# Issuing the tail products of an attention group as one team of eight on TensorE

## The chip, the cores and the metric

The program runs on one core of a Trainium2 chip. The metric is device time in microseconds (us) from one launch; lower is better. TensorE (PE in the profile) does the matrix products, ScalarE (ACT) the Tanh, Exp and copies, VectorE (DVE) additions and conversions, GpSimd (POOL) a little, and SyncE (SP) issues the transfers.

## What is computed

Three stages follow each other. The change is in the first.

```python
# 4 batches, 12 heads, 448 positions, 64 per head
scores = scale * (q @ k.T); scores = cap * tanh(scores / cap)
attn = exp(scores - max) / (sum + 1e-9);  x = attn @ v
...
# second stage: 4 experts, each a causal attention over x, mixed by a gate's top 2
# third stage: x @ w_in, GELU, normalisation, a product over positions, x + gated @ w_out
```

## The kernel before, in words

Heads are worked in 24 **pairs** (4 batches of 6); two pairs are a **group**. Positions 0 to 383 of the keys are three blocks of 128, and 384 to 447 are a tail of 64. Per pair and block, `block` makes the scores (tile `s{b}_{pair}_{c}`, c = 0 to 2): a product for each of the two heads, 64 rows deep and 128 columns wide, side by side on the upper and lower half of TensorE (the profile writes 64\*128). `tails` makes the scores of the tails of a whole group at once (`s{b}_{pair}_3`): four products of 64\*64, one on each quarter of the array. ACT turns scores into probabilities `p`: a Tanh from PSUM, then an Exp in place. `values` multiplies them by v: per pair six products of 128\*64 into `po`, two side by side. The value products of the tails (`po<-p,vt`) are again four of 64\*64: t = 0 on the upper two quarters, into the first pair's `po`, and t = 1 on the lower two, into the second pair's. `sums` adds rows (128\*32).

`slot(i)` records pair i's scores and pair i-1's values. Before the change, the tail scores of group (i, i+1) are the end of `scores(..., 1)` in an even slot i, and the tail values of group (i-2, i-1) stand at the head of `values` for pair i-1, in the same slot. All of it is recorded in the class `Agenda` and issued in an order that a planner makes from fixed costs: `order` takes, step by step, the instruction that can begin first. In slots from 10 on, second-stage work is recorded between the pairs; the first ten slots also prepare w_in (`w2ps` products of 128\*128, fed by VectorE). From pair 12 on the block scores are three single-pass products each (`qh`, `ql`, `kh`, `kl`).

A **team** is a run of recorded PE products of one shape that lie on different cells of the array; the first of them waits until all inputs of the team from outside are there, and has to find buffers for all. The others don't repeat that test (`begin`, lines 275 to 288):

```python
            if i in gang and gang[i][0] == i:
                mates = gang[i]
                wait = first[i]
...
            t = max(t, ready[i])
```

A float32 product is two instructions on PE (two passes), so a row of the profile with x4 is two products. Row names leave buffer numbers out.

Of the kernel before, what the change touches and what calls it, by code (L numbers as in the profile page):

```python
# [10 lines left out]
F32 = mybir.dt.float32  # L11
# [5 lines left out]
AF = mybir.ActivationFunctionType  # L17
# [4 lines left out]
B, H, S, D = 4, 12, 448, 64  # L22
HP = H // 2
# [5 lines left out]
KB, KT = 3, 64  # L29
# [12 lines left out]
def drain(gen):  # L42
    for _ in gen:
        pass
# [32 lines left out]
class Agenda:  # L77


    LATENCY = {"pe": 230.0, "act": 60.0, "dve": 60.0, "pool": 100.0, "sp": 60.0}  # L80
    SLACK, MARGIN = 1000.0, (150.0, 200.0)
    STATE = ("slots", "queue", "where", "left", "free", "grid", "fresh", "cfg", "bank", "lock", "pipe", "kept")
    RULES = ((100.0, 0.0, 100.0), (100.0, 0.0, None), (100.0, 20.0, 100.0), (60.0, 0.0, 100.0))
    OVERLAP = {"act": 100.0, "dve": 80.0, "pool": 27.0, "sp": 0.0}
# [47 lines left out]
    def add(self, eng, f, args, kw):  # L132
        i, name = len(self.ops), f.__name__
# [7 lines left out]
        after, tiles = set(), []  # L141
        for x, wr in [(x, False) for x in ins] + [(x, True) for x in outs]:
            t = x.tensor
# [13 lines left out]
        for these, those in self.behind.items():  # L157
            if any(x.startswith(these) for x in tiles):
                after.update(self.of[those])
        op = dict(i=i, eng=eng, call=lambda: f(*args, **kw), after=after, tiles=set(tiles), took=[], port=False,  # L160
                  rank=i + self.late)
        n = max(x.free_size() for x in ins[:2] + outs[:1])
        psum = any(x.space == PSUM for x in ins + outs)
# [8 lines left out]
        elif eng == "pe":  # L172
            st, mv = (args[1], args[1]) if name == "transpose" else (kw.get("lhsT", args[1]), kw.get("rhs", args[-1]))
            n = mv.free_size() if name != "transpose" else args[1].partition_size()
# [3 lines left out]
            r, c = half(st.partition_size()), half(outs[0].partition_size())  # L178
            if name == "transpose":
                r = c = 4  # L180
# [23 lines left out]
    def order(self, new, by_level, floor):  # L204
        ops, uses = self.ops, self.uses
        then = {i: [] for i in range(len(ops))}
# [3 lines left out]
        for i in reversed(new):  # L210
            op = ops[i]
            took = op["dur"] + self.LATENCY[op["eng"]]
            if "bytes" in op:
                took = 2100.0 + op["extra"] + op["pipe"]
            elif op["eng"] == "pe":
                took = op["dur"] + (0.0 if any(ops[j]["eng"] == "pe" for j in then[i]) else 220.0)
# [4 lines left out]
        for t, u in uses.items():  # L221
            left[t] = len({i for i in u if "end" not in ops[i]}) + (t in keep)
            if t in self.kept and not left[t] and where.get(t, (0, None))[1] is not None:
                key, s = where[t]
                slots[key][s] = max(ops[j]["end"] for j in u)
        self.kept = keep
        for key, tiles in self.caps.items():
# [5 lines left out]
            for t in old:  # L233
                s = next((s for s, v in enumerate(slots[key]) if v is not None), None)
# [24 lines left out]
        gang, team = {}, []  # L259
        for i in new:  # L260
            op = ops[i]
            if op["eng"] != "pe":
                continue
            r, c, r0, c0 = op["cell"]
            if (r, c) == (4, 4) or not team or (r, c) != ops[team[0]]["cell"][:2] or any(
                    abs(r0 - ops[j]["cell"][2]) < r and abs(c0 - ops[j]["cell"][3]) < c for j in team):
                team = []
            team.append(i)
            gang[i] = team
# [46 lines left out]
        while todo:  # L316
            best = None
            for e, pool in pools.items():
# [13 lines left out]
                if e == "pe":  # L332
                    t, i = max(near, key=lambda x: (ops[x[1]]["bank"] == self.bank, ops[x[1]]["key"], -x[1]))
                elif e == "sp":
                    t, i = min(near, key=lambda x: x[1])
                else:
                    t, i = max(near, key=lambda x: (ops[x[1]]["key"], -x[1]))
# [3 lines left out]
            t, i = best  # L341
            op = ops[i]
            e = op["eng"]
            pools[e].remove(i)
            for x in op["tiles"]:
                key, s = where.get(x, (None, 0))
                if s is not None or x not in queue[key]:
                    continue
                s = min((v, k) for k, v in enumerate(slots[key]) if v is not None)[1]
# [4 lines left out]
            if e == "pe":  # L354
                r, c, r0, c0 = op["cell"]
# [25 lines left out]
            for x in op["tiles"]:  # L381
                left[x] -= 1
                if not left[x] and x in where:
                    key, s = where[x]
# [35 lines left out]
def build(ctx: ExitStack, tc: tile.TileContext, a: dict):  # L420
# [145 lines left out]
    def halves(i, c):  # L566
        return (slice(0, S // 2), slice(S // 2, S)) if i == c == 0 else (slice(0, S),)

    def block(s, c, qp, kp, i):

        q, k = parts.get(i, ((qp,), (kp,)))
        of = [(k[0], q[0]), (k[0], q[-1]), (k[-1], q[0])][:1 if len(q) == 1 else 3]
        for n, (y, x) in enumerate(of):
            for o in halves(i, c):
                for j in range(2):
                    r = slice(64 * j, 64 * j + 64)
                    mm(s[:, j, o], y[r, c * 128:(c + 1) * 128], x[r, o], start=(n == 0), stop=(n == len(of) - 1))

    def tails(s, *of):

        for w, (qp, kp) in enumerate(of):
            for j in range(2):
                r = slice(64 * j, 64 * j + 64)
                mm(s[64 * w:64 * w + 64, j, :S], kp[r, KB * 128:S], qp[r, :], start=True, stop=True)

    def scores(b, hp, h, qp, kp, then=None):


        n = 1 if h and then is None else 2
        p = at.tile([128, 2, 2, S], F32, tag="p", name=f"p{b}_{hp}_{h}", bufs=4)
        for c2 in range(n):
            s = ps_s.tile([128, 2, 512], F32, tag="s", name=f"s{b}_{hp}_{2 * h + c2}")
            if 2 * h + c2 < KB:
                block(s, 2 * h + c2, qp, kp, b * HP + hp)
            else:
                tails(s, (qp, kp), then)
            for o in halves(b * HP + hp, 2 * h + c2):
                act.activation(p[:, :, c2, o], s[:, :, o], AF.Tanh, scale=tsc)  # L600
            yield 805.0


        act.activation(p[:, :, :n, :], p[:, :, :n, :], AF.Exp, scale=capt)
        if h == 0:
            pb = at.tile([128, 2, S], F32, tag="pb", name=f"pb{b}_{hp}", bufs=3)
            (dve if (b, hp) < (4, 0) else pool_e).tensor_tensor(pb, p[:, :, 0, :], p[:, :, 1, :], op=ALU.add)
            pend[b, hp] = (p, pb)
        else:
            p0, pb = pend[b, hp]  # L610
            pend[b, hp] = (p0, p, pb)
            if n == 2:
                ptail[b, hp // 2] = p[:, :, 1, :]

    def add_up(b, hp):
# [2 lines left out]
        r = slice(64 * (hp % 2), 64 * (hp % 2) + 64)  # L618
        dve.tensor_tensor(pb[r], pb[r], ptail[b, hp // 2][r], op=ALU.add)

    def values(b, hp, vv):


        i, w = hp // 2, hp % 2
        if w == 0:
            po = ps_o.tile([128, 512], F32, tag="po", name=f"po{b}_{hp}")
            for c in range(KB):
                for j in range(2):
                    mm(po[64 * j:64 * j + 64, :S], vv[:, j, c, :], pend[b, hp][c // 2][:, j, c % 2, :],
                       start=(c == 0), stop=False)  # L630
                yield 805.0
            po_t[b, i] = po
            return
        po = (po_t.pop((b, i)), ps_g.tile([128, 512], F32, tag="g", name=f"po{b}_{hp}"))
        v, p = vt.pop((b, i)), ptail.pop((b, i))
        for t in range(2):
            r = slice(64 * t, 64 * t + 64)
            for j in range(2):
                mm(po[t][64 * j:64 * j + 64, :S], v[r, j, :], p[r, j, :], start=(t == 1), stop=(t == 0))
        yield 805.0  # L640
        os_t[b, i] = ao.tile([128, 2, S], F32, tag="os", name=f"os{b}_{hp}", bufs=5)
        act.activation(os_t[b, i][:, 0, :], po[0][:, :S], AF.Copy)
        for c in range(KB):
            for j in range(2):
                mm(po[1][64 * j:64 * j + 64, :S], vv[:, j, c, :], pend[b, hp][c // 2][:, j, c % 2, :],
                   start=False, stop=(c == KB - 1))
            yield 805.0
        act.activation(os_t[b, i][:, 1, :], po[1][:, :S], AF.Copy)
# [26 lines left out]
    def slot(i, side):  # L675

        if i == 0:
            ld[0] = load_pair(*pairs[0])  # L680
            ld[1] = load_pair(*pairs[1])
        if i + 2 < len(pairs):
            qk = [at.tile([128, n], F32, tag=t, name=f"{t}{i + 2}", bufs=3) for t, n in (("qp", S), ("kp", S + 1))]
            b, hp = pairs[i + 2]
            dma(qk[1][:, :S], a["kT"][b, :, hp, :])
            dma(qk[0], a["qT"][b, :, hp, :])
            ld[i + 2] = qk
        part(i + 1)
        if i < len(pairs):
            first = scores(*pairs[i], 0, *ld[i][:2])  # L690
            drain(islice(first, 2))
            side("a")
            drain(first)
        else:
            side("a")
        side("w")
        if i:
            b, hp = pairs[i - 1]
            drain(values(b, hp, ld.pop(i - 1)[2]))
        if 0 < i < len(pairs) - 1:  # L700
            b, hp = pairs[i + 1]
            ld[i + 1] = (*ld[i + 1], load_v(b, hp))
        side("a")
        if i < len(pairs):
            drain(scores(*pairs[i], 1, *ld[i][:2], None if i % 2 else ld[i + 1][:2]))
        if i == len(pairs):
            drain(sums(B - 1, HP // 2 - 1))
            spread(B - 1, HP // 2 - 1)
        side("p")
        if 0 < i < len(pairs):  # L710
            b, hp = pairs[i - 1]
            if hp % 2 == 1:
                drain(sums(b, hp // 2))
        if i < len(pairs):
            add_up(*pairs[i])
        side("n")
# [726 lines left out]
```

## Time and profile before

| what | us |
|---|---|
| median of 3 runs | 492.72 (492.25 to 493.89) |
| the profiled execution | 492.94 |
| its span, first to last instruction | 491.1 |
| outside the span | 1.84 |
| PE busy | 484.3 (99%) |

The span is what the trace shows; what lies around it stays the same for a kernel with the same launch. PE's granted clock is 1.000 over the span, its full 2.4 GHz.

### The profile page before, as it was taken

The page shows a single profiled execution, that of the slowest core. Times are in us where ns is not written, and L with a number is a line of the kernel's source. Part 1 is how long each engine was busy: PE and PEld are TensorE (multiplying, and loading weights), DVE is VectorE, ACT ScalarE, POOL GpSimd, SP SyncE. Part 2 cuts the span into 40 slices and gives each one's busy share as a digit, 9 for nine tenths or more (in the row PEclk, how much of TensorE's full clock was granted, in tenths as well). Part 3 has the DMA queues.
Part 4 walks back from the last instruction along what each step waited for, and adds up shares of the span by engine and source line. Part 5 has one row for each costly group of instructions (what it writes and reads, how often), then busy time and mean ns, then how long its engine had stood idle before and what let it go on. Part 6 is the DMA issues. An engine that isn't in the chain of part 4 may idle for free.

```text
span 491.1 us, 7664 instructions
## 1 busy us (share of the span) xinstructions
PE 484.3 (99%) x2723; PEld 332.8 (68%) x2723; DVE 362.2 (74%) x796; ACT 325.1 (66%) x555; POOL 47.8 (10%) x61
## 2 busy tenths in 40 slices
PE   9999999999999999999999999999999999999996
PEld 3333333456556657675658797687898998999996
DVE  4999999777899898998756789729979929707000
ACT  6999968999869887788736766647555625513201
POOL 0000000000200303100201302033010200100000
PEclk9999999999999999999999999999999999999999
DMA  8986556555161624141046320161010110110122
GB/s 285 351 308 186 168 133 184 174 151 168 42 176 43 191 61 155 50 131 40 33 128 193 93 81 33 45 240 50 0 39 1 39 37 1 56 57 19 57 75 75
DMA packets 37301, 53.38 MB, mean 109 GB/s; under 512 B 7696, under 2 KB 32272, under 8 KB 37264
## 3 DMA queue, kind: packets, MB, share of 16 engines
q1 hardware_dynamic: 36832, 52.56, 33.9%
q8 instruction: 21, 0.34, 0.3%
q10 hardware_dynamic: 432, 0.34, 0.2%
q14 instruction: 16, 0.13, 0.1%
HBM read 41.97 MB, written 10.83 MB: 108 GB/s over the span
## 4 chain that ended last, share of the span: by engine, by line
PE 90%; DVE 4%; ACT 3%; DMA 1%; issue 1%; SPq 0%; ACTq 0%
PE o L449 18%; PE po L449 12%; PE qk L449 12%; PE s L449 11%; PE sp L449 7%; PE v L449 7%; PE a L449 4%; PE hv L449 4%; PE hu L449 4%; PE w2ps L449 4%; PE av L449 3%; PE tr L449 3%; ACT p L449 2%; PE sum L449 2%; DMA wi_0w<-in_w_in_dram 1%; DVE pb L449 1%
## 5 line engine op out<-in xcount | busy, mean ns | idle before, releaser
L449 ACT ACTIVATE p<-s,tsc 128x896 f32<-128x896 f32 (+1 forms) x85 | 82.3, 999 | 13.1 <-PE s L449 13.0
L449 ACT ACTIVATE p<-p,capt 128x1792 f32<-128x1792 f32 (+1 forms) x48 | 76.9, 1605 | 0.7
L449 PE MATMUL po<-p,vv 128*64 128x448 f32 x288 | 59.9, 548 | 0.1
L449 DVE TENSOR_TENSOR pb<-pb,p 128x896 f32<-128x896 f32 (+1 forms) x48 | 54.1, 1127 | 5.7 <-ACT p L449 5.1
L449 PE MATMUL s<-qp,kp 64*128 64x448 f32 (+2 forms) x244 | 46.4, 566 | 0.2
L449 PEld LDWEIGHTS po<-p,vv 128*64 128x64 f32 x288 | 18.3, 136 | 38.1 <-issue 30.1
L449 DVE CUSTOM_DVE_ANT_0 a<-a,neg 128x128 f32<-128x128 f32 (+3 forms) x56 | 24.7, 471 | 21.3 <-PE a L449 19.2
L449 ACT ACTIVATE ob<-o 128x448 f32<-128x448 f32 (+1 forms) x24 | 12.4, 534 | 37.9 <-PE o L449 34.9
L449 PE MATMUL qk<-xh,wqk_h 128*128 128x448 f32 x96 | 36.5, 380 | 0.1
L449 PEld LDWEIGHTS s<-qp,kp 64*128 64x128 f32 (+1 forms) x244 | 16.4, 171 | 28.0 <-issue 13.5
L449 PE MATMUL qk<-xh,wqk_l 128*128 128x448 f32 x96 | 34.9, 364 | 0.0
L449 ACT ACTIVATE pe<-a,m 128x128 f32<-128x128 f32 (+3 forms) x56 | 27.4, 496 | 9.7 <-DVE m L449 4.9
L449 DVE SCALAR_TENSOR_TENSOR vs<-sp,gln,bsg 128x448 f32<-128x448 f32 x16 | 10.7, 679 | 30.0 <-PE sp L449 29.9
L449 DVE TENSOR_TENSOR pb<-p 128x896 f32<-128x896 f32 x24 | 26.4, 1099 | 7.6 <-ACT p L449 4.8
L449 ACT ACTIVATE gsu<-gsu 128x448 f32<-128x448 f32 x16 | 9.3, 579 | 25.4 <-DVE gsu L449 25.4
L449 PE MATMUL a<-qk 64*128 64x128 f32 (+3 forms) x128 | 25.1, 452 | 0.9 <-ACT qk L449 0.6
L449 PEld LDWEIGHTS qk<-xh,wqk_h 128*128 128x128 f32 x96 | 18.0, 187 | 8.7 <-issue 3.7
L449 PE MATMUL sp<-sg_h,vh 128*128 128x448 f32 x64 | 23.6, 370 | 0.0
L449 PE MATMUL sp<-sg_l,vh 128*128 128x448 f32 x64 | 23.4, 365 | 0.0
L449 PE MATMUL qk<-xl,wqk_h 128*128 128x448 f32 x96 | 22.0, 364 | 0.0
L449 POOL TENSOR_TENSOR rstd<-rstd,mhalf 128x1 f32<-128x1 f32 (+1 forms) x16 | 11.4, 712 | 102.2 <-DVE rstd L449 102.0
L449 PE MATMUL v<-wvg_h,xh 128*128 128x260 f32 x72 | 21.1, 293 | 0.2 <-ACT pe L449 0.2
(272 smaller groups left out, 1200.7 us busy)
## 6 DMA issues: line engine op xcount, KB each, us to landing
rb<-rd SPq DMA_DIRECT2D x24, 224.0 KB, 4.2
kp<-in_kT_dram SPq DMA_DIRECT2D x23, 224.0 KB, 4.0
qp<-in_qT_dram SPq DMA_DIRECT2D x23, 224.0 KB, 4.2
out_dram<-ob SPq DMA_DIRECT2D x23, 224.0 KB, 1.9
vv<-in_v_dram SPq DMA_DIRECT2D x24, 192.0 KB, 3.5
wuw<-in_w_out_dram SPq DMA_DIRECT2D x5, 384.0 KB, 4.2
wud<-wuw SPq DMA_DIRECT2D x10, 192.0 KB, 3.6
ws<-in_wqk_dram SPq DMA_DIRECT2D x4, 384.0 KB, 5.5
```

What stands on the lines that cost most here:

```text
L449: return tc.keep_in_program_order(f(*args, **kw))
```

## The change

The tail value products move out of `values` into `tail_values`, and the tail scores out of `scores` into `tail_scores`; in every even slot `slot` records both, one behind the other, ahead of the values of pair i-1. While they are recorded, a mark `agenda.join` is set, and products with the same mark go into one team even where their cells overlap. So a team has up to eight products instead of four.

```diff
-            if (r, c) == (4, 4) or not team or (r, c) != ops[team[0]]["cell"][:2] or any(
+            if (r, c) == (4, 4) or not team or (r, c) != ops[team[0]]["cell"][:2] or (
+                    op["join"] is None or op["join"] != ops[team[0]]["join"]) and any(
                     abs(r0 - ops[j]["cell"][2]) < r and abs(c0 - ops[j]["cell"][3]) < c for j in team):
                 team = []
...
+    def tail_scores(i):
+        early[i] = new_p(*pairs[i], 1)
+        tanh(i, KB, early[i], ld[i][:2], ld[i + 1][:2])
...
+    def tail_values(b, i):
+        po = (po_t[b, i], ps_g.tile([128, 512], F32, tag="g", name=f"po{b}_{2 * i + 1}"))
+        v, p = vt.pop((b, i)), ptail.pop((b, i))
+        for t in range(2):
+            r = slice(64 * t, 64 * t + 64)
+            for j in range(2):
+                mm(po[t][64 * j:64 * j + 64, :S], v[r, j, :], p[r, j, :], start=(t == 1), stop=(t == 0))
...
+        if i % 2 == 0:
+            agenda.join = f"t{i}"
+            if i:
+                tail_values(pairs[i - 1][0], pairs[i - 1][1] // 2)
+            if i < len(pairs) and i:
+                tail_scores(i)
+            agenda.join = None
         side("w")
```

What the planner makes of it, on PE in slots 1 and 2 (batch 0; `vt` are the tails' values, `s0_2_3` the tail scores). Before:

```order
L449 MATMUL po0_0_141<-p0_0_1_129,vv0_0_113 64x448 x2
L449 MATMUL po0_0_141<-p0_0_1_129,vt0_0_114 64x448 x2
L449 MATMUL po0_1_156<-p0_0_1_129,vt0_0_114 64x448 x2
L449 MATMUL s0_1_2_145<-qp0_1_115,kp0_1_116 128x448 x2
...
L449 MATMUL s0_2_1_150<-qp2_118,kp2_119 128x448 x2
L449 MATMUL s0_2_2_160<-qp2_118,kp2_119 128x448 x2
L449 MATMUL po0_1_156<-p0_1_0_134,vv0_1_117 64x448 x4
L449 MATMUL po0_1_156<-p0_1_1_144,vv0_1_117 64x448 x2
L449 MATMUL s0_2_3_161<-qp2_118,kp2_119 64x448 x2
L449 MATMUL s0_2_3_161<-qp3_132,kp3_133 64x448 x2
```

With the change:

```order
L451 MATMUL po0_0_141<-p0_0_1_129,vv0_0_113 64x448 x2
L451 MATMUL po0_1_154<-p0_0_1_129,vt0_0_114 64x448 x2
L451 MATMUL s0_1_2_145<-qp0_1_115,kp0_1_116 128x448 x2
...
L451 MATMUL s0_2_1_150<-qp2_118,kp2_119 128x448 x2
L451 MATMUL po0_0_141<-p0_0_1_129,vt0_0_114 64x448 x2
L451 MATMUL s0_2_3_157<-qp2_118,kp2_119 64x448 x2
L451 MATMUL s0_2_3_157<-qp3_132,kp3_133 64x448 x2
L451 MATMUL po0_1_154<-p0_1_0_134,vv0_1_117 64x448 x4
```

The two t = 1 products (into `po0_1`) stay where the four stood; the two t = 0 products (into `po0_0`) move to the tail scores, which stand ahead of the second pair's values now.

PE in slot 16 (batch 2, pair 4). Before:

```order
L449 MATMUL po2_2_965<-p2_2_1_944,vt2_2_912 64x448 x2
L449 MATMUL po2_3_998<-p2_2_1_944,vt2_2_912 64x448 x2
L449 MATMUL s2_4_3_1009<-qp16_930,kp16_931 64x448 x2
L449 MATMUL s2_4_3_1009<-qp17_954,kp17_955 64x448 x2
L449 MATMUL po2_3_998<-p2_3_0_960,vv2_3_943 64x448 x4
```

With the change:

```order
L451 MATMUL po2_3_994<-p2_2_1_942,vt2_2_912 64x448 x2
L451 MATMUL s2_4_3_997<-qp16_930,kp16_931 64x448 x2
L451 MATMUL s2_4_3_997<-qp17_954,kp17_955 64x448 x2
L451 MATMUL po2_2_965<-p2_2_1_942,vt2_2_912 64x448 x2
L451 MATMUL po2_3_994<-p2_3_0_960,vv2_3_945 64x448 x4
```

All eight stood together already; now the t = 1 products come first, then the tail scores, then the t = 0 products.

ACT in slots 4 and 5 with the change (`tsc` is Tanh, `capt` Exp, `os` and `w2h` copies, `wi10m` a conversion step):

```order
L451 ACTIVATE p0_4_0_187<-s0_4_1_189,tsc_70 128x2x448
L451 ACTIVATE w2h0_1_224<-w2ps0_1_163 128x512
L451 ACTIVATE p0_4_0_187<-p0_4_0_187,capt_69 128x1792
L451 ACTIVATE os0_3_194<-po0_2_177 128x448
L451 ACTIVATE p0_4_1_195<-s0_4_3_196,tsc_70 128x2x448
L451 ACTIVATE os0_3_194<-po0_3_193 128x448
L451 ACTIVATE p0_4_1_195<-s0_4_2_200,tsc_70 128x2x448
L451 ACTIVATE wi10m_259<-wi1_4w_212 128x512
L451 ACTIVATE p0_4_1_195<-p0_4_1_195,capt_69 128x1792
```

Before, the Tanh of `s0_4_2` stood ahead of the first Exp, and the Tanh of the tail scores `s0_4_3` right ahead of the second; now the tail scores' Tanh comes first and that of `s0_4_2` last.

How the 64\*64 tail products stand on PE, by even slot (VT the four tail values, ST the four tail scores, t0 and t1 the two halves of VT; "/" parts visits, with other shapes between):

| slots | before | with the change |
|---|---|---|
| 2, 4, 6, 10 | VT / ST | t1 / t0 ST |
| 8 | ST VT | t1 / t0 ST |
| 12 | VT ST | ST / VT |
| 14, 20 | VT / ST | VT ST |
| 16, 22 | VT ST | t1 ST t0 |
| 18 | VT ST | VT ST |

Counted over the program, PE changes from one shape to another 154 times before (27 of these runs are 64\*64) and 151 with the change (27 again): one run of 64\*128, one of 128\*64 and one of 128\*128 fewer. From slot 24 on, every engine's order is as before, and no engine has an instruction more or less.

## Rows read from the trace of the kernel before

**Rows 1.** Page, busy time of each engine over the span.

```profile
PE 484.3 (99%) x2723; PEld 332.8 (68%) x2723; DVE 362.2 (74%) x796; ACT 325.1 (66%) x555; POOL 47.8 (10%) x61
```

**Rows 2.** Stretches of the span: length, busy time of each engine, clock, DMA.

```profile
10.00:25.00 15.00, 14.87 (x70) 5.25 (x72) 14.73 (x26) 14.78 (x16) 0.00 (x0) 1.00 1.03 359
25.00:50.00 25.00, 24.90 (x124) 8.23 (x124) 24.70 (x43) 24.27 (x28) 0.00 (x0) 1.00 0.72 236
```

**Rows 3.** PE's timeline, slots 1 and 2: start, length, operation, shape.

```profile
13.63 0.97 PE L449 MATMUL po<-p,vv 128*64 128x448 f32 x4
14.54 0.98 PE L449 MATMUL po<-p,vt 64*64 64x448 f32 x8
15.45 1.77 PE L449 MATMUL s<-qp,kp 64*128 64x448 f32 x8
17.15 1.12 PE L449 MATMUL w2ps<-wi0m,wt 128*128 128x512 f32 x2
18.12 1.02 PE L449 MATMUL w2ps<-wi1m,wt 128*128 128x512 f32 x2
18.98 1.02 PE L449 MATMUL w2ps<-wi0m,wt 128*128 128x512 f32 x2
...
20.79 1.77 PE L449 MATMUL s<-qp,kp 64*128 64x448 f32 x8
22.49 2.48 PE L449 MATMUL po<-p,vv 128*64 128x448 f32 x12
24.89 0.98 PE L449 MATMUL s<-qp,kp 64*64 64x448 f32 x8
25.81 1.72 PE L449 MATMUL po<-p,vv 128*64 128x448 f32 x8
```

**Rows 4.** PE's timeline in slot 8, tail scores and tail values adjacent.

```profile
78.37 0.98 PE L449 MATMUL s<-qp,kp 64*64 64x448 f32 x8
79.17 0.93 PE L449 MATMUL po<-p,vt 64*64 64x448 f32 x8
80.03 3.98 PE L449 MATMUL po<-p,vv 128*64 128x448 f32 x20
```

**Rows 5.** PE's timeline, two 64*64 products alone (second stage).

```profile
126.85 0.97 PE L449 MATMUL a<-qk 64*64 64x448 f32 x4
127.75 0.48 PE L449 MATMUL s<-qh,kh 64*128 64x448 f32 x2
```

**Rows 6.** All engines' timeline, slot 3: PE waits for ACT; [idle before <-releaser].

```profile
31.28 0.70 DVE L449 TENSOR_TENSOR wi4m<-wi4m,wi4e 128x512 f32<-128x512 f32 x1
...
31.87 2.14 PE L449 MATMUL s<-qp,kp 64*128 64x448 f32 x8
...
32.99 0.30 PEld L449 LDWEIGHTS s<-qp,kp 64*128 64x128 f32 x4 [0.82 <-ACT p L449]
...
33.95 1.12 PE L449 MATMUL w2ps<-wi2m,wt 128*128 128x512 f32 x2
```

**Rows 7.** ACT's timeline, slots 4 to 6.

```profile
41.27 1.00 ACT L449 ACTIVATE p<-s,tsc 128x896 f32<-128x896 f32 x1
42.16 1.79 ACT L449 ACTIVATE p<-p,capt 128x1792 f32<-128x1792 f32 x1
43.84 0.54 ACT L449 ACTIVATE os<-po 128x448 f32<-128x448 f32 x1
...
52.37 0.60 ACT L449 ACTIVATE w2h<-w2ps 128x512 fp32r<-128x512 f32 x1
52.84 0.56 ACT L449 ACTIVATE os<-po 128x448 f32<-128x448 f32 x1
53.27 0.62 ACT L449 ACTIVATE w2h<-w2ps 128x512 fp32r<-128x512 f32 x1
53.74 0.71 ACT L449 ACTIVATE wi10m<-wi_4w 128x512 f32<-128x512 f32 x1
```

**Rows 8.** SP's timeline, the load of pair 3's q; page, DMA issues: us to landing.

```profile
15.32 0.33 SPq L449 DMA_DIRECT2D qp<-in_qT_dram  x1
...
qp<-in_qT_dram SPq DMA_DIRECT2D x23, 224.0 KB, 4.2
```

More of the change, by code (lines that the diff above doesn't have):

```diff
@@ L81 @@
     SLACK, MARGIN = 1000.0, (150.0, 200.0)
+    join = None
     STATE = ("slots", "queue", "where", "left", "free", "grid", "fresh", "cfg", "bank", "lock", "pipe", "kept")
@@ L159, in add @@
                 after.update(self.of[those])
-        op = dict(i=i, eng=eng, call=lambda: f(*args, **kw), after=after, tiles=set(tiles), took=[], port=False,
+        op = dict(i=i, join=self.join, eng=eng, call=lambda: f(*args, **kw), after=after, tiles=set(tiles), took=[], port=False,
                   rank=i + self.late)
@@ L586, in tails, with tanh, new_p, scores @@
                 mm(s[64 * w:64 * w + 64, j, :S], kp[r, KB * 128:S], qp[r, :], start=True, stop=True)
[L588 to L600, printed above, removed]
+    def tanh(i, c, p, *of):
+        s = ps_s.tile([128, 2, 512], F32, tag="s", name=f"s{i // HP}_{i % HP}_{c}")
+        if c < KB:
+            block(s, c, *of, i)
+        else:
+            tails(s, *of)
+        for o in halves(i, c):
+            act.activation(p[:, :, c % 2, o], s[:, :, o], AF.Tanh, scale=tsc)
+    early = {}
+    def new_p(b, hp, h):
+        return at.tile([128, 2, 2, S], F32, tag="p", name=f"p{b}_{hp}_{h}", bufs=4)
+    def tail_scores(i):
+        early[i] = new_p(*pairs[i], 1)
+        tanh(i, KB, early[i], ld[i][:2], ld[i + 1][:2])
+    def scores(b, hp, h, qp, kp):
+        i = b * HP + hp
+        n = 1 if h and i and i not in early else 2
+        p = early.pop(i) if h and i in early else new_p(b, hp, h)
+        for c in range(2 * h, min(2 * h + 2, KB + (i == 0))):
+            tanh(i, c, p, *((qp, kp) if c < KB else ((qp, kp), ld[i + 1][:2])))
             yield 805.0
@@ L619, in add_up @@
         dve.tensor_tensor(pb[r], pb[r], ptail[b, hp // 2][r], op=ALU.add)
+    def tail_values(b, i):
[5 more added lines that the diff above has]
+                mm(po[t][64 * j:64 * j + 64, :S], v[r, j, :], p[r, j, :], start=(t == 1), stop=(t == 0))
+        os_t[b, i] = ao.tile([128, 2, S], F32, tag="os", name=f"os{b}_{2 * i + 1}", bufs=5)
+        act.activation(os_t[b, i][:, 0, :], po[0][:, :S], AF.Copy)
+        po_t[b, i] = po
     def values(b, hp, vv):
@@ L633, in values @@
             return
[L634 to L642, printed above, removed]
+        po = po_t.pop((b, i))
         for c in range(KB):
@@ L704, in slot @@
         if i < len(pairs):
-            drain(scores(*pairs[i], 1, *ld[i][:2], None if i % 2 else ld[i + 1][:2]))
+            drain(scores(*pairs[i], 1, *ld[i][:2]))
         if i == len(pairs):
```

## The prediction

> **What bounds the kernel now.** I read the page's busy times first: PE is busy for 484.3 of 491.1 us, far above every other engine [rows 1]. A busy PE may still be one that waits with work in hand, so I then read PE's timeline and took times from start to start, each visit to one product shape until the next visit begins. They are regular enough to be a price list [rows 3]. I call a **round** what runs side by side on the parts of the array, each product with its two passes. A visit of three rounds of 128\*64 takes 2.40 us (22.49 to 24.89), one round 0.91 (13.63 to 14.54): a round is (2.40 - 0.91) / 2 = 0.75, and 0.16 go with entering the shape. Four tail products on the four quarters are one round as well: 0.91 (14.54 to 15.45) and 0.92 (24.89 to 25.81). Two rounds of 64\*128 take 1.70, so that entry is 0.20; four w2ps products take 3.64 (17.15 to 20.79) at 0.86 each, entry 0.20. These visits have next to nothing left over, so PE's own sequence sets the pace from slot 1 on. But the margins are thin at the start: between 10 and 50 us ACT is busy for 39.05 of 40 us and DVE for 39.43 [rows 2]. PE does wait there: the scores at 31.87 take 2.08 until the next visit instead of 1.70, for a Tanh [rows 6].
>
> So the change is to be priced in PE's rounds and entries, slot by slot, and then in waits for ACT and DVE.
>
> **Fewer entries.** If eight products stand together, they pay one entry: tail scores and tail values in slot 8 take 1.66 for two rounds [rows 4], where two separate visits take 0.91 + 0.92 [rows 3]. That is the gain to be had, 0.16 or so at a place. But five of the eleven slots have it already (8, 12, 16, 18, 22), and the order with the change shows it newly at two only (14, 20), while slots 8 and 12 lose it. The 64\*64 visits stay 27. Elsewhere the order has one visit fewer of each of three shapes: 0.20 (64\*128) + 0.16 (128\*64) + 0.20 (128\*128) = **0.56 saved**.
>
> **Split teams.** Only the team's first product waits for the others' inputs. The t = 1 products need the same probabilities as t = 0, but they open a buffer of their own and come second: now that the first has to wait for the tail scores' operands and buffer too, they go without it. In slots 2, 4, 6, 8 and 10 they stand alone, two products on the two lower quarters. What two products on two of four quarters cost the trace shows: 0.90 [rows 5], no less than four. Later the t = 0 products and the tail scores share a visit, but not a round: t = 0 holds the upper quarters, and the tail scores need all four. That is two rounds. So there are three rounds for eight products where there were two: +0.75 in each of five slots, **3.75**.
>
> **The order t = 1, tail scores, t = 0** (slots 16 and 22). No row shows a visit in which an earlier product waits for its quarter while a later one has its own free; [rows 4] keep all quarters equally full. Upwards it is three rounds: the first tail score starts beside t = 1 on the upper left, the second wants the lower left and waits, the third and fourth are behind it, and the last t = 0 product has to wait for the third. Downwards it is two rounds, as before, when free quarters are filled out of turn. I take three, since products start in the order's sequence in every row here ([rows 3] follow the listing of the change line by line): +0.75 each, **1.50**, with 0 as the other end. The Trainium skill (TensorE: Matmul & The Clock Gate, Part 3, The mechanism) says that matmuls start and end in program order and that only weight loads are pulled ahead; by that the 1.50 stand, and without it they would be 0. No run here shows it.
>
> **Waits.** The t = 1 products, the tail scores and their Tanh come earlier, the third block's scores later, and w2ps goes past them. In slots 4 and 5, from the end of the scores `s0_4_1`, PE's order has the values of pair 3 (2.40), t = 0 with the tail scores (1.66), one block of scores (0.75 + 0.20), the sums (one round, taken at 0.91 like the others), two rounds of values (1.66) and two of scores (1.70) [rows 3, 4], 9.28 us, and then takes the second Exp. ACT's listed work to that Exp is three Tanh at 0.89, two Exp at 1.68, a w2h copy of 0.47, two os copies of 0.43 and a conversion step of 0.71 [rows 7], 8.07 us. The slack is 1.2 us, less what ACT has still in hand when the stretch begins, which in so full a stretch can be a whole Exp. DVE: PE now comes to the w2ps block of slot 3 at 20.79 + 0.95 + 1.66 + five rounds with entry (3.91) + 0.91 + 1.70 = 29.9 instead of 33.95, and to its third input 1.7 later, at 31.6; before, that input was finished at 31.98 [rows 6], though DVE takes it earlier in its order now. Both say: a few tenths here or there. Bounds: below, the wait that is there goes, 2.08 - 1.70 = 0.38 [rows 6]; above, one such wait in each of the five split slots, 1.9. I take **+0.4**, near the row that exists.
>
> **At nothing.** No instruction and no transfer is added on any queue. SP issues the same transfers in another order; the q and k of the next pair, which the tail scores need sooner, are issued a slot ahead: pair 3's q at 15.32, so that with 4.2 us to landing it is there at 19.5 [rows 8]. PE wanted it at 24.89 [rows 3] and now wants it at 20.79 + 0.95 + 0.75 + 0.16 = 22.65, so the visits between cover it by 3 us; with that cover gone, PE would wait for up to the 4.2 us of a landing. The os copy from `po` goes behind another Tanh on ACT; the next user of that buffer is the values of the next group, for which the sum over slots 4 and 5 above stands. From slot 24 on all orders are the same, and there the loss is only carried along: PE has no idle time there in which it could vanish.
>
> **Sum.** 3.75 + 1.50 - 0.56 + 0.4 = 5.1 us. The profiled execution took 492.94, 0.2 over the median of 492.72. From that median: **497.8**.
>
> **Rivals.**
> 1. *Free quarters are filled out of turn*, so slots 16 and 22 cost nothing: 497.8 - 1.5 = 496.3. For it: four products do run at once on four quarters. Against it: products start in sequence in all rows. Chance 0.13. The Trainium skill (TensorEngine Tiling (Array Packing), Key Properties) says that tiles operate independently and that different tiles can run matmuls in parallel; read to the letter, that is this rival, and its time 496.3. No row here shows it.
> 2. *ACT becomes late.* One wait of 0.38 in each of the five split slots, 1.9 in place of 0.4: 499.3. For it: ACT's full stretches [rows 2] and the slack of 1.2 us. Against it: PE gets slower by 0.75 in each of these slots, which gives ACT that much time. It decides as soon as ACT carries more than 1.2 us into such a stretch. Chance 0.14.
> 3. *Not slower: a half-filled visit costs only the quarters that it fills.* While t = 1 holds the lower half, the next visit's products on the upper half (`s0_1_2` in slot 1) begin. Then the third rounds vanish, and 492.72 - 0.56 = 492.2 is left. It needs the next shape to begin before the visit's two passes end. Against it: after two products on two quarters the next shape starts 0.90 later [rows 5], and every change of shape in [rows 3] costs 0.16 to 0.20. Chance 0.03. The Trainium skill (TensorEngine Tiling (Array Packing), Key Properties) says that a change of tiling mode drains the array; the trace agrees, with those 0.16 to 0.20 at each entry.
> 4. *It does what it says*, eight products together in all eleven slots: six entries fewer, 492.72 - 0.56 - 6 x 0.16 = 491.2. The order denies it: it shows five such teams, two of them out of sequence. Chance 0.01.
>
> **How the numbers follow.** The forecast, 497.8, has 0.66; rivals 0.31; 0.03 is left for what I have not seen, above all an order in which a wait of several us hides. The range goes from 492.72 + 3.75 - 0.56 - 0.38 = 495.5 (rival 1 with the old wait gone) up to rival 2's 499.3 and a little more for other waits: 495.5 to 500.0. A change of under 0.3%, 1.5 us, can hardly be told from none in a measurement of this kernel. Slower by more: forecast, rivals 1 and 2 and most of the rest, 0.95. Within 0.3%: rival 3 and a forecast of which most is given back elsewhere, 0.03. Faster: 0.02 (rival 4 and the unseen).
>
> **What would show it.** In slots 2 to 10: `po<-p,vt` x4 alone, about 0.90 to the next visit, and a 64\*64 visit of x12 of about 1.66; in slots 16 and 22 a visit of x16 at 2.4 instead of 1.66; in 14 and 20 one of 1.66. Between slots 1 and 12 PE should fall back by about 3.5 us against the old trace, by slot 24 by 5, and then keep that distance. ACT and DVE keep their busy times, PE's grows by about 5. Wrong I am if the x4 visits end in clearly less than 0.9, if the x16 visits take 1.66, or if PE shows waits for ACT of over 2 us in sum before 100 us.

## The result, and the profile after

Paired with runs of the kernel before on the same chip (median 493.31 us), the changed kernel has a median of **498.66 us** (497.62 to 499.63, 4 runs): a ratio of **1.0106, interval 1.0091 to 1.0121**, or 4.5 to 6.0 us more. Its profiled execution took 499.05 us, 6.1 over the profiled one of before. Of all the executions behind the medians below, one of run 4 took 695.8 us, at a granted clock of 0.656, and the ratio of run 4 is taken from the other three. The first lines of its page answer to [rows 1]:

```profile
span 497.3 us, 7664 instructions
...
PE 488.6 (98%) x2723; PEld 334.9 (67%) x2723; DVE 361.7 (73%) x796; ACT 324.8 (65%) x555; POOL 48.3 (10%) x61
```

The instructions are as many as before, ACT and DVE are as busy within 0.5 us, and PE is busy for 4.3 us more; the span has grown by 6.2. So some 4 us stand in the trace as work of PE, done in a worse form, and the rest is waiting. PE's timeline of slots 1 and 2 shows both (start, length, operation, shape, and in brackets an idle time and what ended it); it answers to [rows 3]:

```profile
13.59 0.97 PE L451 MATMUL po<-p,vv 128*64 128x448 f32 x4
14.49 0.97 PE L451 MATMUL po<-p,vt 64*64 64x448 f32 x4
15.39 1.77 PE L451 MATMUL s<-qp,kp 64*128 64x448 f32 x8
...
20.82 1.02 PE L451 MATMUL s<-qp,kp 64*128 64x448 f32 x4
21.77 0.59 PE L451 MATMUL po<-p,vt 64*64 64x448 f32 x2
21.79 0.60 PE L451 MATMUL s<-qp,kp 64*64 64x448 f32 x2
22.20 0.54 PE L451 MATMUL po<-p,vt 64*64 64x448 f32 x2
22.21 1.27 PE L451 MATMUL s<-qp,kp 64*64 64x448 f32 x6
23.42 2.48 PE L451 MATMUL po<-p,vv 128*64 128x448 f32 x12
26.94 1.72 PE L451 MATMUL po<-p,vv 128*64 128x448 f32 x8 [1.04 <-ACT p L451]
```

The two t = 1 products (the row with x4) stand alone at 14.49 and take 0.90 until the next shape, as much as four. The visit that follows at 21.77, t = 0 with the tail scores, takes 1.65. Slots 4, 6, 8 and 10 show the same pair of visits, 0.90 and 1.65 in each. In slots 14 and 20 the eight stand together in 1.66. Slot 16 is the odd one:

```profile
159.48 0.59 PE L451 MATMUL po<-p,vt 64*64 64x448 f32 x2
159.82 0.59 PE L451 MATMUL s<-qp,kp 64*64 64x448 f32 x1
159.91 0.54 PE L451 MATMUL po<-p,vt 64*64 64x448 f32 x2
159.93 0.93 PE L451 MATMUL s<-qp,kp 64*64 64x448 f32 x5
160.62 0.54 PE L451 MATMUL po<-p,vt 64*64 64x448 f32 x1
160.66 0.54 PE L451 MATMUL s<-qp,kp 64*64 64x448 f32 x2
160.71 0.91 PE L451 MATMUL po<-p,vt 64*64 64x448 f32 x3
161.55 0.97 PE L451 MATMUL po<-p,vv 128*64 128x448 f32 x4
```

It takes 2.07, as does slot 22 at 231.16: 0.41 more than two rounds with an entry, neither the 0.75 that I had taken nor 0. The tail scores are not kept waiting by the order: one starts at 159.82, ahead of the second pass of t = 1 at 159.91, which stands before it in the order. What it waited for before that is in ACT's timeline, a score buffer that the first of these two Tanh sets free about when half of their 1.91 us is over, near 159.7:

```profile
158.76 1.91 ACT L451 ACTIVATE p<-s,tsc 128x896 f32<-128x896 f32 x2 [0.21 <-PE s L451]
```

The waits of this execution, PE's by what released them:

```profile
PE po L451 <- ACT p L451: 1.4, 2, 1.0
PE warm L451 <- DVE tsc L451: 1.0, 1, 1.0
PE a L451 <- ACT qk L451: 0.6, 1, 0.6
PE tr L451 <- DVE ri L451: 0.5, 1, 0.5
```

The 1.4 are two: the one at 26.94 above, and 0.34 at 53.33. The second and third row stand in the list of the kernel before with the same times, the first and fourth do not. Start to start, the visits with a wait are longer than their rounds and entry by 1.25 (23.42), 0.41 (51.21), 0.41 (196.83) and 0.39 (202.32); the old one of [rows 6] is gone (-0.37), and so is one of 0.20 in slot 1 of before; the first slot ends 0.16 later, on a load. That is +2.05.

So the 6.1 of these two executions: 5 x 0.75 for the split teams, 2 x 0.41 for slots 16 and 22, -0.56 for the entries and +2.05 of waits, 6.06. The medians differ by 5.35; below, the 1.25 turns out to hang on the landing of a load, and not on the order alone.

### The profile page after: what moved, and what is told of

The parts are those of the page before. It is cut to its first block, busy times and chain, and to the rows that moved or that the text cites. A ratio compares the mean times of both kernels' runs of the same rounds, so it can differ in the third digit from the quotient of the medians.

```text
span 497.3 us, 7664 instructions
## 1 busy us (share of the span) xinstructions
PE 488.6 (98%) x2723; PEld 334.9 (67%) x2723; DVE 361.7 (73%) x796; ACT 324.8 (65%) x555; POOL 48.3 (10%) x61
## 4 chain that ended last, share of the span: by engine, by line
PE 90%; DMA 4%; ACT 2%; DVE 2%; issue 1%; SPq 0%; DVEq 0%; ACTq 0%
PE o L451 18%; PE po L451 13%; PE qk L451 12%; PE s L451 10%; PE sp L451 7%; PE v L451 7%; PE a L451 4%; PE hv L451 4%; PE hu L451 4%; PE w2ps L451 3%; PE av L451 3%; PE tr L451 3%; PE sum L451 2%; ACT p L451 2%; DMA wt<-in_woT_dram 1%; DMA wi_5w<-in_w_in_dram 1%
## 5 line engine op out<-in xcount | busy, mean ns | idle before, releaser
L451 DVE TENSOR_TENSOR pb<-pb,p 128x896 f32<-128x896 f32 (+1 forms) x48 | 53.0, 1103 | 13.2 <-ACT p L451 12.6
L451 PE MATMUL s<-qp,kp 64*128 64x448 f32 (+2 forms) x244 | 50.4, 562 | 0.6 <-ACT p L451 0.4
L451 PEld LDWEIGHTS s<-qp,kp 64*128 64x128 f32 (+1 forms) x244 | 18.0, 171 | 26.7 <-issue 14.7
```

What stands on the lines that cost most here:

```text
L451: return tc.keep_in_program_order(f(*args, **kw))
```

## The experiments

My theory: the loss is the third round of the split teams, and behind it stands the early place of the tail scores, for which the planner splits them. Rival theories: holding eight products together costs as much in waits; products keep the order's sequence (so the split is not the point); a half-filled visit is cheap. The times are medians; the kernel before had 493.34 beside the first four runs and 492.76 beside the last four.

**1. Eight together in all slots.** In `begin`, a product of a marked team may not go before the team's first.

```diff
+            if i in gang and ops[i]["join"] and gang[i][0] != i and "end" not in ops[gang[i][0]]:
+                return None
             t = max(t, ready[i])
```

> The change, but no product of a marked team may go before the team's first one, so the eight tail products stand together in all eleven even slots (four value tails, then four tail scores). PE's order has 145 visits (154 before, 151 with the change), 21 of them 64*64. Theory (a split team costs a round of 0.75 us, a visit an entry of 0.16 to 0.20): the five x4 visits are gone, every team is one x16 visit of 1.66, and the loss goes with them: 1.4 us less than the kernel before plus what PE waits for ACT, so 491.5 to 494. Rival (the loss is waiting for ACT that comes with the tail scores' early place, not the split): the x16 visits are there, but the time stays 3 us or more over the kernel before, with PE waits for p in the first 60 us. Slots 16 and 22: if their 2.07 comes from the wait of the tail scores for a Tanh, which four value tails in front now cover, they take 1.66; if it comes from the order of the products, also 1.66, so this run alone doesn't tell these two apart.

Measured: 498.91 us, ratio 1.0106 (1.0087 to 1.0125), no better than the change. Nine visits fewer than before, 145 instead of 154, should have given back 1.44 us; 5.57 were lost, so some 7 us of waits have come in. PE's timeline shows the largest, in slot 2:

```profile
17.79 0.98 PE L453 MATMUL po<-p,vt 64*64 64x448 f32 x8
20.34 1.08 PE L453 MATMUL s<-qp,kp 64*64 64x448 f32 x8 [1.57 <-ACT p L453]
21.35 2.48 PE L453 MATMUL po<-p,vv 128*64 128x448 f32 x12
```

and the list of PE's waits the kind:

```profile
PE s L453 <- ACT p L453: 3.4, 4, 1.6
...
PE s L453 <- DMA qp<-in_qT_dram: 0.8, 1, 0.8
```

The tail scores, put right behind the tail values, stand there until a Tanh has emptied a score buffer. The theory's expectation was wrong, and the rival's came true: in sum, the split is a price paid in place of such waits, not on top of them. Only 2.9 of the 7 us stand in the teams' own visits (1.90, 0.62 and 0.37 over 1.66 in slots 2, 6 and 10); the rest is spread over other visits. In slots 16 and 22 the team takes 1.67 and 1.76 here, with its products in the order t = 0, t = 1, scores.

**2. Eight together, recorded t = 1, tail scores, t = 0.** The edit above, and `tail_values` takes t in the order 1, 0 with the tail scores between:

```diff
-        for t in range(2):
+        for t in (1, 0):
...
+            if t and then is not None:
+                tail_scores(then)
```

> As the whole team, but recorded as the t = 1 products, the tail scores, the t = 0 products, in all eleven even slots. 144 visits, 21 of them 64*64. If products on a quarter that is busy hold up those behind them (in order), each team is three rounds, 2.41 per x16 visit, 6.6 us over the kernel before: 500. If free quarters are filled out of turn, each team is two rounds, 1.66 wherever the tail scores' buffer is free at once, and up to 0.4 more where they wait for a Tanh; the time is then within 1 us of the whole team's.

Measured: 501.79 us, ratio 1.0182 (1.0155 to 1.021). The time is 2.9 over run 1's, where I had allowed 1 for free quarters filled out of turn, and by itself it would fit the strict order's 500 better. So the visit has to decide. Slot 14:

```profile
138.66 0.59 PE L453 MATMUL po<-p,vt 64*64 64x448 f32 x2
138.68 0.60 PE L453 MATMUL s<-qp,kp 64*64 64x448 f32 x2
139.09 0.54 PE L453 MATMUL po<-p,vt 64*64 64x448 f32 x2
139.10 0.91 PE L453 MATMUL s<-qp,kp 64*64 64x448 f32 x4
139.48 0.55 PE L453 MATMUL po<-p,vt 64*64 64x448 f32 x2
139.84 0.54 PE L453 MATMUL s<-qp,kp 64*64 64x448 f32 x2
139.85 0.55 PE L453 MATMUL po<-p,vt 64*64 64x448 f32 x2
140.33 0.60 PE L453 MATMUL po<-p,vv 128*64 128x448 f32 x2
```

138.66 to 140.33 is 1.67, two rounds with an entry, in an order that in strict sequence needs three (2.41). Slots 4, 8 and 18 have 1.67 as well; slots 12, 16 and 22 have 2.06 to 2.07, the 0.41 of the changed kernel, slot 20 has 1.85, and slots 2, 6 and 10 have 2.7 to 4.3, with waits. So a free quarter is filled out of turn: the mechanism of my first rival holds, and the 0.41 is a wait for the score buffer. What is lost in time is waits, some 10 us with the 1.64 of the ten entries saved.

**3. The moved places without the mark.** The change with teams of four as before:

```diff
-            agenda.join = f"t{i}"
+            agenda.join = None
```

> The change's places for tail values and tail scores, without the mark: two teams of four, next to each other or not as the planner finds. 151 visits as with the change, 27 of them 64*64, but no team is split. Theory: the five third rounds and the 0.4 in slots 16 and 22 are gone, so 0.56 us less than the kernel before plus waits: 492 to 494. Rival (the moved places cost, by ACT being late): 3 us or more over the kernel before.

Measured: 495.29 us, ratio 1.004 (1.0026 to 1.0054), between what I had written for the theory and for the rival. No team is split, 151 visits, 0.56 less by entries, and still 2 us more: 2.5 us of waits. So the moved places alone cost 2.0 us, and the mark, which is all that this run lacks, 498.66 - 495.29 = 3.4.

```profile
PE po L451 <- ACT p L451: 1.8, 4, 1.1
...
PE tr L451 <- ACT vp L451: 0.4, 1, 0.4
```

**4. Half-filled visits in the kernel before.** The t = 1 products go behind the first block's values of the later pair, in `values`, so that the four tail products of a group no longer share a round: two and two stand apart, in a visit of their own or beside other 64\*64 products.

```diff
-        for t in range(2):
+        def tail(t):
             r = slice(64 * t, 64 * t + 64)
             for j in range(2):
-                mm(po[t][64 * j:64 * j + 64, :S], v[r, j, :], p[r, j, :], start=(t == 1), stop=(t == 0))
+                mm(po[t][64 * j:64 * j + 64, :S], v[r, j, :], p[r, j, :], start=False, stop=(t == 0))
+        tail(0)
...
-                   start=False, stop=(c == KB - 1))
+                   start=(c == 0), stop=(c == KB - 1))
+            if c == 0:
+                tail(1)
```

> The kernel before with the suspected cost doubled: in values, the t = 1 products of the tails are recorded behind the first block's products of the second pair instead of right behind t = 0, so that in all twelve groups the tail values are two half-filled teams. 171 visits instead of 154. Theory (a half-filled visit costs a whole round and an entry): twelve more rounds of 0.75 and 17 more entries, 2.6 us in sum, 11.6 us over the kernel before: 504 to 506. Rival (a half-filled visit costs only what it fills, the next shape begins beside it): only the entries, under 3 us.

Measured: 505.2 us, ratio 1.023 (1.0204 to 1.0256), 11.9 more against the 11.6 expected of twelve more rounds and their entries. Two visits of two products in slot 1:

```profile
14.22 0.97 PE L449 MATMUL po<-p,vt 64*64 64x448 f32 x4
15.12 1.77 PE L449 MATMUL s<-qp,kp 64*128 64x448 f32 x8
17.51 0.97 PE L449 MATMUL po<-p,vv 128*64 128x448 f32 x4 [0.61 <-ACT p L449]
18.41 0.97 PE L449 MATMUL po<-p,vt 64*64 64x448 f32 x4
19.31 1.90 PE L449 MATMUL po<-p,vv 128*64 128x448 f32 x8
```

14.22 to 15.12 and 18.41 to 19.31, 0.90 each. A half-filled visit costs a whole one; the rival that it is cheap falls.

**5. Eight together in slots 12 to 22 alone.** The edit of run 1, and in slots 2 to 10 the tails as before the change.

```diff
-        if i % 2 == 0:
+        if i % 2 == 0 and i >= 12:
             agenda.join = f"t{i}"
```

> The teams of eight, held together, in slots 12 to 22 alone; slots 2 to 10 as in the kernel before. 149 visits instead of 154, none of them a round more: 0.84 us less by the entries (five of 0.16 to 0.20). Theory (the loss lies where ScalarE's Tanhs stand close, ahead of slot 12): nearly nothing against it, at most the 0.45 and 0.30 that the run with eight together showed behind slot 12: 492.2 to 493.4 against 493.3 of before, and every visit of sixteen at about 1.66. Rival (the early place costs a wait in any slot): 1 us and more of waits, 494 to 496.

Measured: 493.78 us, ratio 1.0014 (0.9999 to 1.0029): no difference that can be told, and no gain shown. All six late teams take 1.66 to 1.76, five entries are saved (0.84), and what comes in their place is a handful of short waits, for example

```profile
PE tr L453 <- ACT qk L453: 0.4, 1, 0.4
PE tr L453 <- ACT vp L453: 0.4, 1, 0.4
PE v L453 <- ACT pe L453: 0.2, 1, 0.2
```

between 100 and 240 us, where the list of before has a single row, 0.2 for `qk`. Neither theory is cleanly met: the time lies between their ranges, and the waits are spread over the chain of the second stage instead of standing before the tail scores.

**6. The change in slots 2 to 10 alone.** The change as it is, with the opposite condition (`i < 12`).

> The change in slots 2 to 10 alone; from slot 12 on the kernel before. 156 visits, five half-filled rounds more than before: 3.75 of rounds and 0.32 of entries, 4.07 together, and the waits that the changed kernel showed in these slots (1.25 and 0.41 more, 0.57 less): 5.2. Theory (the loss lies ahead of slot 12): 497.8 to 499.0, nearly all of the changed kernel's. Rival (a good part comes from the later slots, 16 and 22 among them): 496 to 497.3.

Measured: 496.7 us, ratio 1.0076 (1.0058 to 1.0095), 3.9 more than before; the rounds and entries alone were to be 4.07. So the waits of these slots come to nothing in sum, and the loss of these slots is the split teams. My range (from 497.8) was too high by the waits that I had carried over from one execution. This run shows why: up to slot 10 its orders on PE, ACT, DVE and SP are those of the changed kernel, so its first 90 us or so are a second execution of it. In ACT's timeline the conversion step that waits for its load starts at 21.42, and nothing behind it is late:

```profile
21.42 0.69 ACT L451 ACTIVATE wi5m<-wi_5w 128x512 f32<-128x512 f32 x1 [0.38 <-DMA wi_5w<-in_w_in_dram]
```

where the changed kernel's profiled execution had

```profile
23.21 0.67 ACT L451 ACTIVATE wi5m<-wi_5w 128x512 f32<-128x512 f32 x1 [1.69 <-DMA wi_5w<-in_w_in_dram]
23.78 0.99 ACT L451 ACTIVATE p<-s,tsc 128x896 f32<-128x896 f32 x1
```

with the Tanh for the values at 26.94 behind it. The same transfer landed at 21.34 in one and at 23.12 in the other. SP's timeline has its issue, first in run 6 and then in the changed kernel:

```profile
15.87 0.38 SPq L451 DMA_DIRECT2D wi_5w<-in_w_in_dram  x1
...
16.64 0.38 SPq L451 DMA_DIRECT2D wi_5w<-in_w_in_dram  x1
```

Of the 1.78 between the landings, 0.77 is a later issue and 1.0 a longer way, 6.5 us from issue to landing in place of 5.5. So the 1.25 at 23.42 does not come with the order alone. How often the changed kernel has it is not shown: one execution of it was profiled. The 0.41 at 51.21 comes again here (0.40 at 49.44), and the wait of [rows 6] is gone here too.

**7. Eight together at the tail scores' old place.** The hold of run 1, but the tail values come down to the end of the slot and close both accumulators there:

```diff
+            if c == KB:
+                agenda.join = f"t{i}"
+                if i:
+                    tail_values(pairs[i - 1][0], pairs[i - 1][1] // 2)
             tanh(i, c, p, *((qp, kp) if c < KB else ((qp, kp), ld[i + 1][:2])))
+            agenda.join = None
```

> The team of eight held together, but at the end of the slot, where the tail scores stand in the kernel before: the tail values come down to them and close both accumulators. 144 visits, no split round: 1.72 us less than before by the entries. Theory (what made the team dear is the tail scores' early place, where they ask for a score buffer and ScalarE that the blocks still use): few waits, 491.3 to 492.8. Rival (it is holding eight products back for one another that costs, at any place): 3 to 5 us of waits, 495 to 498.

Measured: 495.37 us, ratio 1.0055 (1.0036 to 1.0073). Ten entries fewer, 1.72 us, and 2.6 lost: 4.3 of waits. My theory of the place falls, and the rival's range is met: with the tail scores where they were, waits come all the same, and other ones. The profiled execution took 496.89, 1.5 over the median, so not each of its waits need stand in the others. From PE's list:

```profile
PE v L453 <- DVE pt L453: 1.8, 1, 1.8
PE s L453 <- DMA qp<-in_qT_dram: 1.5, 1, 1.5
PE po L453 <- ACT p L453: 1.1, 3, 0.7
PE s L453 <- ACT p L453: 1.0, 1, 1.0
```

The 1.5 is the load of the first slot, which differs from execution to execution, as seen above; the others are ACT and DVE.

**8. One conversion step moved from ACT to DVE**, the one that stood before the wait of 1.25.

```diff
-            p, e = from64(raw.pop(u), m, e, act if u > 1 else dve)
+            p, e = from64(raw.pop(u), m, e, act if u > 1 and u != 5 else dve)
```

> The changed kernel with one Abs of the weight conversion, the one of the sixth slice, on VectorE instead of ScalarE; no visit of TensorE differs. Theory (the 5.17 us visit at 23.4 is long because ScalarE, in order, stands behind that Abs, which waits for its load to land): the visit falls back to about 3.9 us, 497.2 to 498.2 in all. Rival (it is the score buffer and the Tanh that are late there, the Abs is only near by): the visit stays at about 5.2, 498.3 to 499.3.

Measured: 498.4 us, ratio 1.0113 (1.0094 to 1.0132): nothing gained. The wait of slot 2 is gone, as expected (the values run through, 24.34, x20). Run 6 shows that it can be gone without the edit, when the load lands early; here it landed late again, at 23.10, 1.24 behind the end of ACT's step before it (1.60 in the changed kernel), and ACT, rid of the step, stood ready for the Tanh and waited for PE:

```profile
22.81 1.01 ACT L451 ACTIVATE p<-s,tsc 128x896 f32<-128x896 f32 x1 [0.95 <-PE s L451]
```

So the chain from the load over ACT to PE is as the theory has it, and a late landing is no matter of a single execution. But one wait of DVE's stands before the visit now, and the visit at 50.89 has grown by 0.45:

```profile
18.97 0.70 PE L451 MATMUL w2ps<-wi1m,wt 128*128 128x512 f32 x1 [0.57 <-DVE wi1m L451]
...
24.34 3.98 PE L451 MATMUL po<-p,vv 128*64 128x448 f32 x20
```

## Why the prediction was right, and which terms were not

The time was right, 498.66 for 497.8 and inside the range, and so was the cause in the main. Term by term:

- **Split teams, 3.75: right.** 0.90 for the x4 visits and 1.65 for the x12 visits in slots 2 to 10, as written. Run 6 has this part of the change by itself: 3.9 measured, 4.07 by rounds and entries. Run 3, which lacks the mark alone, is 3.4 faster than the change, with more waits. Run 4 confirms the price of a half-filled visit from the other side. It is most of the loss.
- **The order t = 1, tail scores, t = 0, 1.50: wrong.** The step that failed is "I take three, since products start in the order's sequence". They do not where a quarter is free (159.82 before 159.91; 1.67 in run 2). Slot 2 shows it too: two tail scores start at 21.79, ahead of the second passes of t = 0 at 22.20. Had nothing else been there, rival 1's 0 would have stood. The visits are longer by 0.41 each, 0.82 in all, for the score buffer. The Trainium skill's rule that I had put behind this step (TensorE: Matmul & The Clock Gate, Part 3, The mechanism: matmuls start in program order) does not hold for these rows: by it, the visit of run 2 would take 2.41. The one behind rival 1 (TensorEngine Tiling (Array Packing), Key Properties: tiles operate independently) does, with 1.67.
- **Entries, -0.56: right.** 151 visits; the other shapes' rounds kept their prices of [rows 3].
- **Waits, +0.4: too small.** In the profiled execution they were +2.05. The 1.25 hangs on a landing that differs from execution to execution, and so does the 0.16 of the first slot; the 0.20 of slot 1 is there again in run 6 (0.25). Without these three it is 0.41 + 0.41 + 0.39 - 0.37 = 0.84. With these terms the sum is 3.75 + 0.82 - 0.56 + 0.84 = 4.85, inside the measured 4.5 to 6.0. The 0.50 that is left to the 5.35 between the medians is open: the 1.25 in a part of the executions would fill it, which is not shown. So two errors in size went against each other, 0.68 too much for the order and 0.44 too little for the waits, and that 5.1 came so near is in part luck. Ahead of slot 12 PE was 5.19 behind (the `qk` products at 105.57 before and at 110.76 with the change) where I had written about 3.5; the 1.25 and the 0.41 at 51.21 are most of that. A slip in the working: by [rows 3] the third w2ps input is wanted 1.83 behind the visit's start (17.15 to 18.98), not 1.7; nothing hangs on it.
- **At nothing: right, but for the 0.16 of the first slot.** The loss stayed as it was from slot 24 to the end (6.1 us behind the old trace at the third expert's products, 6.13 at PE's last one), and ACT and DVE kept their busy times. PE's wait for ACT from slot 1 to 100 us was 1.4, under the 2 that would have spoken against me.
- **Rivals.** 1: right as to the mechanism, wrong as to the time, since the visit waits for something else. 2: the waits it counts on did not come in each split slot (run 6: none in sum). 3: falls with run 4. 4: the order denied it, and run 1 shows that it would not have helped.

What stays open is why every order without split teams that I ran brings some 2 to 10 us of waits with it (runs 1, 2, 3, 5 and 7: 7.0, some 10, 2.5, some 1.8 and 4.3). The rows name ACT's Tanh most often, but in run 7 also DVE, in run 5 the second stage's chain. No run was faster than the kernel before.

## What to carry to other kernels

Where a scheduler tests only a group's first member, a larger group can come out as smaller visits: count visits and rounds in the issued order, not in the code that records it. Price a half-filled visit as a full one. An entry saved at 0.16 to 0.20 us pays only if the engines that feed the new order keep up with it, and in runs 1, 2, 3, 5 and 7 they did not. The busy share does not tell where: between 10 and 50 us ACT and DVE are busy for all but 1 us of 40, but run 5's waits came between 100 and 240 us, where in the kernel before ACT is busy for 117.4 and DVE for 122.1 of 140 us.

## What the runs showed that I had not expected

- Products on a free quarter start before earlier ones whose quarter is taken: eight in the order t = 1, scores, t = 0 took 1.67, as long as in the order t = 0, t = 1, scores.
- One execution can differ from another in a single wait of over a microsecond, with the same order on PE, ACT, DVE and SP: a transfer landed at 21.34 in one and at 23.12 in the other, 1.0 of it by a longer way from issue to landing, and PE's 1.04 of waiting for ACT was there in the second alone. What one profile shows as a wait for ACT need not be the kernel's; the row on ACT that ended on a DMA was the hint.
